# Sparse attention with a gated MLP on one core: the first half's global V rows by transfers, zeroing on GpSimd, casts on VectorE, and a changed order and banks around the first AV products

## The chip, the core and the metric

The kernel runs on one core of a Trainium2 chip. The metric is the device time of one execution in microseconds (us). Ten executions of the kernel before gave a median of 238.23 us (237.54 to 239.25).

## The reference

Two things are computed one after the other. First an attention over 4 batches, 8 heads, 768 positions and a head width of 64, in which a position sees the first 8 keys (the global ones) and the 96 keys up to itself, with a bias that falls with distance and has a slope of its own for each head. Then a gated MLP over the 3,072 resulting rows of width 512.

```python
scores = scale * np.matmul(q, k.transpose(0, 1, 3, 2))
is_global = pos[None, :] < n_global                      # 8
is_local = (rel >= 0) & (rel < n_local)                  # 96
dist = np.where(is_global & ~is_local, n_local, np.abs(rel))
scores = np.where(is_global | is_local, scores - slopes * dist, -1e9)
a = softmax(scores)
x = np.matmul(a, v)                                      # then (B*S, H*D)
out = (np.maximum(x @ w_gate, 0) * (x @ w_val)) @ w_out  # 512 -> 1536 -> 512
```

## The kernel before, in words

**Tiling.** The work is cut into eight half batches of 384 queries, numbered s = 0 to 7 in the code (`NHALF`). Each has four head pairs p = 0 to 3. The keys of a batch are held in seven blocks j of 128 columns: 8 global keys, the same in every block, and 120 local ones. A first half (s even) needs blocks 0 to 3, a second half blocks 2 to 6. `vbuf` holds V in the same blocks with keys on partitions: partitions 0 to 7 hold the global rows of V, repeated in every block, and partitions 8 to 127 the block's own rows.

**Stages of a half.** `piece_cast` (L258) turns q and k from fp32 to bf16. `piece_t` (L288) transposes them on TensorE. `piece_copy_k` and `piece_copy_q` (L304, L312) bring the transposed keys and queries from PSUM to `kT` and `qT`. `piece_bias` (L319) puts the bias into three PSUM banks by a matmul, `piece_scores` (L334) adds the scores, and `piece_exp` (L348) takes the exponential on ScalarE. `piece_av_wide` (L454) makes two products: the sums of the weights (with a tile of ones, `what` = 0), and then the weights times V (`what` = 1). `piece_ln_wide` and `piece_inverse_wide` (L481, L486) make the reciprocal of the sums as exp(-ln) on ScalarE. `piece_mul_wide` (L491) multiplies on VectorE into `xT`. The MLP reads `xT`: `gate` and `val` (L748, L756) are its first two matmuls with weights `wg` and `wv`, followed by a third product with `wo`.

**What sets the order.** The schedule is manual: every engine executes its instructions in the order in which the program calls the pieces, and waits by semaphores on what it reads and on the buffers that it overwrites. For the first two halves the order is written out by hand, from L834 to L977; from L978 on, lists of pieces are woven between the MLP's matmuls. PSUM has three pools: `qk` with 3 banks, `av` with 2 and `ff` with 3 (L76 to L78). A bank can be written again when its last reader is done. `rc_pool` (L70) has two buffers each for the logarithms and the reciprocals, so the fourth pair's reciprocal waits until the second pair's has been used.

**Queues.** SyncE issues the fp32 loads of q and k for the first half at once (L177). GpSimd issues all loads that cast to bf16: the global V rows (`load_v_globals`, L140), V blocks (`load_v`, L152), q and k of the second half (`load_qk_cast`, L126), and the weights (`load_w`, L170). It issues them in program order among its memsets.

**The places that the change touches.** `copy_v_globals` (L148) spreads the global rows of V over the blocks by VectorE copies, in two calls; it is used in the first batch only. For the later batches `spread_v_globals` (L144) does the same by six small transfers within SBUF, issued by SyncE (8 partitions x 8 heads x 64 elements each). `zero_values` (L205) zeroes partitions 32 to 127 of V's block 3 for the first batch, as only 24 of its rows are loaded early. The first AV product with its ln and inverse stands after the exponentials of the last head pair (L880, L881), the second half's first transposes after the third AV product (L904), and a second half's copies after the fourth (L907).

Of the kernel before, what the change touches and what calls it, by code (L numbers as in the profile page):

```python
# [16 lines left out]
def kernel(  # L17
# [12 lines left out]
    nc = tc.nc  # L30
# [15 lines left out]
    NT = -(-S // KT)  # L46
# [79 lines left out]
    def load_qk_cast(s, h0=0, h1=H):  # L126

        b, half = divmod(s, 2)
        for i, src in ((1, k), (0, q)):
            qk16[s, i] = kc[i].rearrange("p n d -> p (n d)").rearrange("p (h x) -> p h x", h=H)  # L130
            nc.gpsimd.dma_start(
                out=qk16[s, i][:, h0:h1],
                in_=src[b, h0:h1, half * QH : (half + 1) * QH, :].rearrange(
                    "h (p n) d -> p h (n d)", n=NN))

    def v_dst(b, r0, r1, j):
        t = vbuf[b % 2][r0:r1, j, D:]
        return t.rearrange("p (h z) -> p h z", z=2 * D)[:, :, 0:D]
# [5 lines left out]
    def spread_v_globals(b, j0=1, j1=NT):  # L144
        for j in range(j0, j1):
            nc.sync.dma_start(out=v_dst(b, 0, NG, j), in_=v_dst(b, 0, NG, 0))

    def copy_v_globals(eng, b, j0, j1):  # L148
        t = vbuf[b % 2][0:NG, :, D:].rearrange("p j (h z) -> p j h z", z=2 * D)[:, :, :, 0:D]
        eng.tensor_copy(t[:, j0:j1], t[:, 0:1].to_broadcast([NG, j1 - j0, H, D]))  # L150

    def load_v(b, j, r0=0, r1=KT):  # L152
        n = min(r1, S - KT * j) - r0
        nc.gpsimd.dma_start(  # L154
            out=v_dst(b, NG + r0, NG + r0 + n, j),
            in_=v[b, :, KT * j + r0 : KT * j + r0 + n, :].rearrange("h p d -> p h d"))
# [13 lines left out]
    def load_w(dst, src, f0, f1):  # L170
        nc.gpsimd.dma_start(out=dst, in_=src[:, f0:f1].rearrange("(c p) f -> p c f", p=128))
# [29 lines left out]
    def zero_keys():  # L201
        for p in range(1, HP):
            nc.vector.memset(kT[0][p][:, 3, 32:128], 0.0)

    def zero_values():  # L205
        for r0, r1 in ((32, 64), (64, 128)):
            nc.vector.memset(v_dst(0, r0, r1, 3), 0.0)

# [35 lines left out]
    def warm_up(n):  # L246
        wps = ff_psum.tile([128, 512], FP32, name="ff_ps")
        for _ in range(n):
            nc.tensor.matmul(wps, lhsT=warm, rhs=warm.unsqueeze(1).to_broadcast([128, 4, 128]), start=True, stop=True)

    QKB, FFB, AVB = (qk_psum, "qk_ps"), (ff_psum, "ff_ps"), (av_psum, "av_ps")
# [6 lines left out]
    def piece_cast(s, p, i, eng):  # L258
        if (s, p) not in cast_of:
            cast_of[s, p] = oflat[:, 384 * p : 384 * (p + 1)].bitcast(BF16).rearrange(  # L260
                "t (i n e d) -> t i n e d", i=2, n=NN, e=2)
        src = (qs_of[s], ks_of[s])[i]
        (eng.copy if eng is nc.scalar else eng.tensor_copy)(
            cast_of[s, p][:, i].rearrange("t n e d -> t e n d"),
            src[:, 2 * p : 2 * p + 2, :].rearrange("t e (n d) -> t e n d", n=NN))
# [22 lines left out]
    def piece_t(s, p, pool=av_psum, name="av_ps", apart=False):  # L288
        for i in (1, 0):
            if i == 1 or apart:  # L290
                tp = pool.tile([128, 512], FP32, name=name)
                tp = tp[:, 0:QH].bitcast(BF16).rearrange("d (i t) -> d i t", i=2)
            tp_of[s, p, i] = tp[:, i, :]
            for n in range(NN):
                for e in range(2 if s == 1 else 1):
                    r = slice(64 * e, 64 * e + 64) if s == 1 else slice(0, 128)
                    src = (qk16[s, i][:, 2 * p + e, n * D : (n + 1) * D] if s == 1
                           else cast_of[s, p][:, i, n])
                    nc.tensor.matmul(tp[r, i, n * 128 : (n + 1) * 128],  # L299
                                     lhsT=src, rhs=ident, is_transpose=True,  # L300
                                     start=((i == 1 or apart) and n == 0),
                                     stop=((i == 0 or apart) and n == NN - 1))

    def piece_copy_k(s, p):  # L304
        b, half = divmod(s, 2)
        put_keys(nc.vector.tensor_copy, nc.vector.tensor_copy, kT[b % 2][p], tp_of[s, p, 1], half)

    def piece_copy(s, p):
        piece_copy_k(s, p)
        piece_copy_q(s, p)  # L310

    def piece_copy_q(s, p, copy=nc.vector.tensor_copy):  # L312
        for e in range(2):
            r = slice(64 * e, 64 * e + 64)
            copy(qTb[s % 2][r, p, e, :], tp_of[s, p, 0][r, :])
# [45 lines left out]
    def piece_biased(s, p):  # L361
        piece_scores(s, p)
        for g in range(3):
            piece_exp(s, p, g)
# [89 lines left out]
    def piece_av_wide(s, p, *pools):  # L454

        b, half = divmod(s, 2)
        todo = [t for bank in banks_of_half[half] for t in bank]
        pools = pools or (AVB,)
        av = [pool.tile([128, 512], FP32, name=name) for pool, name in (pools[0], pools[-1])]
        for what in range(2):  # L460
            av3 = av[what][:, 0:QH].rearrange("d (n p) -> d n p", n=NN)
            for i, (j, a, w, m) in enumerate(todo):
                for e in range(2):
                    es, ce = es_of[s, p, j, e]
                    z0 = D + 2 * D * (2 * p + e)
                    nc.tensor.matmul(av3[64 * e : 64 * e + 64, :, a : a + w],  # L466
                                     lhsT=ones if what == 0 else vbuf[b % 2][:, j, z0 : z0 + D],
                                     rhs=es[:, ce : ce + NN * w].rearrange("k (n p) -> k n p", n=NN),
                                     start=(i == 0), stop=(i == len(todo) - 1),
                                     skip_group_check=True)  # L470
        av_of[s, p] = av
# [5 lines left out]
    def piece_sums_wide(s, p):  # L477
        piece_ln_wide(s, p)
        piece_inverse_wide(s, p)

    def piece_ln_wide(s, p):  # L481
        ln = rc_pool.tile([128, QH], FP32, name="lnd")
        nc.scalar.activation(ln, av_of[s, p][0][:, 0:QH], AF.Ln, bias=0.0, scale=1.0)
        av_of[s, p, "l"] = ln

    def piece_inverse_wide(s, p):  # L486
        rc = rc_pool.tile([128, QH], FP32, name="rcp")
        nc.scalar.activation(rc, av_of[s, p, "l"], AF.Exp, bias=0.0, scale=-1.0)
        av_of[s, p, "r"] = rc

    def piece_mul_wide(s, p):  # L491
        if s not in xT_of:
            xT_of[s] = xt_pool.tile([128, N_DC, QH], BF16, name="xT")
        nc.vector.tensor_tensor(xT_of[s][:, p, :], av_of[s, p][1][:, 0:QH], av_of[s, p, "r"], op=ALU.mult)
# [327 lines left out]
    def cast(s, p, ek, eq):  # L822
        piece_cast(s, p, 1, ek)
        piece_cast(s, p, 0, eq)

    V, P, A = nc.vector, nc.gpsimd, nc.scalar
# [14 lines left out]
    for j in range(3):  # L841
        load_v(0, j)
    load_v(0, 3, 0, 24)
    load_qk_cast(1, 0, H // 2)
    for f in (0, 256):
        load_w(wg[0][:, :, f : f + 256], moe_w_gate, f, f + 256)
    load_qk_cast(1, H // 2, H)
    load_w(wv[0], moe_w_val, 0, GW * 128)
    warm_up(7)
    cast(0, 0, V, V)  # L850
    piece_t(0, 0, apart=True)
    piece_bias(0, 0)
# [1 line left out]
    piece_copy_k(0, 0)  # L854
    piece_copy_q(0, 0, nc.scalar.copy)
    zero_keys()
    zero_values()
    cast(0, 1, A, V)
    piece_scores(0, 0)
    piece_t(0, 1)  # L860
    piece_bias(0, 1)
    piece_exp(0, 0, 0)
    cast(0, 2, A, A)
    piece_exp(0, 0, 1)
    piece_exp(0, 0, 2)
    piece_copy(0, 1)
    piece_t(0, 2)
    cast(0, 3, A, A)
    piece_biased(0, 1)
    piece_bias(0, 2, (0, 1))  # L870
    piece_copy(0, 2)
# [2 lines left out]
    piece_biased(0, 2)  # L874
    piece_copy(0, 3)
    piece_bias(0, 3)
    copy_v_globals(V, 0, 1, 4)
    piece_biased(0, 3)
    copy_v_globals(V, 0, 4, NT)
    piece_av_wide(0, 0, QKB)  # L880
    piece_sums_wide(0, 0)  # L881

    zero_q(P, 1)
    for p in range(HP):
# [9 lines left out]
        piece_copy(s, p)  # L894

    gate, val = F0[0:8:2], F0[1:8:2]
    piece_av_wide(0, 1)
    piece_ln_wide(0, 1)
    piece_av_wide(0, 2, FFB)
    piece_ln_wide(0, 2)  # L900
    piece_mul_wide(0, 0)
    piece_inverse_wide(0, 1)
    piece_inverse_wide(0, 2)
    piece_t(1, 0, *QKB)  # L904
    piece_av_wide(0, 3, QKB, FFB)
    piece_ln_wide(0, 3)
    piece_copy(1, 0)  # L907
    piece_mul_wide(0, 1)
    piece_inverse_wide(0, 3)
    piece_t(1, 1)  # L910
    piece_bias(1, 0)
    piece_mul_wide(0, 2)
    piece_mul_wide(0, 3)
    piece_copy(1, 1)
    for h in (3, 4):
# [123 lines left out]
```

## Time and profile before

| what | us |
|---|---|
| median of ten executions | 238.23 |
| the profiled execution | 239.25 |
| its span | 237.4 |
| TensorE (PE) busy in the span | 231.0 (97%) |
| VectorE (DVE) busy | 188.1 (79%) |
| ScalarE (ACT) busy | 146.2 (62%) |
| GpSimd (POOL) busy | 90.4 (38%) |
| granted TensorE clock | full in all 40 slices |
| DMA moved | 30.43 MB, mean 128 GB/s |

The profile is one execution; its own time is the span and what lies around it (1.85 us). An engine's busy time is an average over stages with different limits: the stage that the change touches is the first 31 us. In the first 4 us TensorE is busy for 3.0 us, and from 16 to 18 us for 1.39 of 2 us. In the rows of a timeline the first number is the start within the span, the second the length, and brackets hold the idle time before the row and what ended it. POOLq and SPq are the queues that issue transfers; q0 is the DMA queue of GpSimd's transfers and q1 that of SyncE's. A share of 100% in a DMA row means all 16 DMA engines; it can be above that, since packets overlap on an engine.

### The profile page before, as it was taken

What the parts mean: (1) busy time and instruction counts of PE and PEld (TensorE: products, weight loads), DVE (VectorE), ACT (ScalarE), POOL (GpSimd) and SP (SyncE); (2) the same over time, 40 slices, a digit from 0 to 9 for tenths busy, and PEclk for the clock granted to TensorE, in tenths of its full rate; (3) what the DMA queues carried; (4) which work ended last, traced back from release to release, by engine and by line L of the source; (5) the groups of instructions that cost most, each with busy time, mean ns of one, the idle gap of its engine ahead of it and who ended that gap; (6) DMA issues with size and microseconds to landing.
All of it is one profiled execution on the core that took longest, in us unless ns stands there. A gap on an engine that the chain in (4) does not pass through costs nothing.

```text
span 237.4 us, 5510 instructions
## 1 busy us (share of the span) xinstructions
PE 231.0 (97%) x2021; PEld 159.2 (67%) x2021; DVE 188.1 (79%) x466; ACT 146.2 (62%) x321; POOL 90.4 (38%) x191
## 2 busy tenths in 40 slices
PE   7989999999999999999999999999999999999994
PEld 3776666656677666856688566856688666865683
DVE  5688767869977878976989788876889777873784
ACT  6899875667623887567842687558742687624310
POOL 8998903933565065606580065505150000000000
PEclk9999999999999999999999999999999999999999
DMA  6999999998469974767398664847712200020005
GB/s 170 201 167 183 206 270 274 169 109 266 46 134 188 169 246 95 64 160 227 90 77 123 189 204 105 53 125 244 78 45 88 91 0 3 0 91 0 1 3 177
DMA packets 71419, 30.43 MB, mean 128 GB/s; under 512 B 47744, under 2 KB 70784, under 8 KB 71392
## 3 DMA queue, kind: packets, MB, share of 16 engines
q0 software_dynamic: 34896, 10.27, 38.9%
q1 hardware_dynamic: 36496, 19.82, 30.7%
q8 instruction: 16, 0.26, 0.5%
q14 instruction: 11, 0.09, 0.1%
HBM read 28.38 MB, written 6.29 MB: 146 GB/s over the span
## 4 chain that ended last, share of the span: by engine, by line
PE 85%; ACT 6%; DVE 5%; DMA 1%; issue 1%; SPq 0%; DVEq 0%; ACTq 0%
PE ff_ps L744 50%; PE ff_ps L632 19%; PE av_ps L431 5%; PE ff_ps L777 2%; PE av_ps L513 2%; PE qk_ps L513 2%; DVE obuf L643 1%; DMA qs<-in_q_dram 1%; PE av_ps L299 1%; PE qk_ps L344 1%; DVE xT L451 1%; ACT grelu L753 1%; ACT rcp L445 1%; PE av_ps L466 1%; ACT lnd L440 1%
## 5 line engine op out<-in xcount | busy, mean ns | idle before, releaser
L753 ACT ACTIVATE grelu<-ff_ps 128x384 bf16<-128x384 f32 x96 | 46.8, 490 | 53.2 <-PE ff_ps L744 40.8
L744 PE MATMUL ff_ps<-xT,wv 128*128 128x384 bf16 x384 | 77.9, 326 | 0.0
L744 PE MATMUL ff_ps<-xT,wg 128*128 128x384 bf16 x384 | 77.7, 326 | 0.1
L760 DVE TENSOR_TENSOR ht<-ff_ps,grelu 128x384 f16<-128x384 f32 x96 | 53.3, 556 | 25.4 <-PE ff_ps L744 22.0
L744 PEld LDWEIGHTS <-wv 128*128 128x128 bf16 x384 | 36.0, 98 | 23.7 <-issue 1.2
L744 PEld LDWEIGHTS <-wg 128*128 128x128 bf16 x384 | 36.4, 97 | 21.8 <-issue 1.4
L451 DVE TENSOR_TENSOR xT<-av_ps,rcp 64x384 bf16<-64x384 f32 x48 | 26.6, 555 | 7.7 <-ACT rcp L445 6.7
L367 POOL CAST kc<-ks 128x384 bf16<-128x384 f32 x20 | 10.8, 583 | 53.7 <-DMA ks<-in_k_dram 53.7
L534 DVE TENSOR_TENSOR es<-es,m_all 128x432 bf16<-128x432 bf16 (+3 forms) x108 | 30.7, 328 | 0.2 <-ACT es L522 0.2
L643 DVE TENSOR_TENSOR obuf<-ff_ps,obuf 128x512 f32<-128x512 f32 (+1 forms) x46 | 27.6, 603 | 3.7 <-PE ff_ps L632 0.9
L440 ACT ACTIVATE lnd<-av_ps 64x384 f32<-64x384 f32 x48 | 23.3, 485 | 11.3 <-PE av_ps L431 10.5
L522 ACT ACTIVATE es<-qk_ps 128x432 bf16<-128x432 f32 (+2 forms) x54 | 27.6, 531 | 0.0
L154 POOL DMA_DIRECT2D vbuf<-in_v_dram x29 | 24.8, 864 | 0.1
L431 PE MATMUL av_ps<-es,vbuf 128*128 128x216 bf16 (+4 forms) x216 | 21.4, 226 | 0.2 <-DVE xT L451 0.2
L431 PEld LDWEIGHTS <-vbuf 128*128 128x128 bf16 x216 | 18.2, 98 | 5.0 <-issue 0.3
L632 PEld LDWEIGHTS <-ht 128*128 128x128 f16 x198 | 18.6, 97 | 3.9 <-issue 0.8
L632 PEld LDWEIGHTS <-hsum 128*128 128x128 f16 x192 | 18.5, 98 | 2.1
L632 PE MATMUL ff_ps<-wo_sb,ht 128*128 128x256 f16 x132 | 19.3, 272 | 0.0
L632 PE MATMUL ff_ps<-wo_sum,hsum 128*128 128x256 f16 x144 | 17.2, 273 | 0.0
L445 ACT ACTIVATE rcp<-lnd 128x384 f32<-128x384 f32 x24 | 12.6, 523 | 0.8
L367 POOL CAST qc<-qs 128x384 bf16<-128x384 f32 x20 | 10.5, 568 | 0.7 <-DMA qs<-in_q_dram 0.5
L522 ACT ACTIVATE es<-av_ps 128x432 bf16<-128x432 f32 (+2 forms) x18 | 9.5, 528 | 1.8 <-PE qk_ps L513 1.8
(130 smaller groups left out, 265.4 us busy)
## 6 DMA issues: line engine op xcount, KB each, us to landing
out_dram<-obuf SPq DMA_DIRECT2D x22, 256.0 KB
ks<-in_k_dram SPq DMA_DIRECT2D x5, 768.0 KB
qs<-in_q_dram SPq DMA_DIRECT2D x5, 768.0 KB
vbuf<-in_v_dram POOLq DMA_DIRECT2D x23, 120.0 KB, 4.6
wv<-in_moe_w_val_dram POOLq DMA_DIRECT2D x3, 512.0 KB, 10.2
wo_sb<-in_moe_w_out_dram POOLq DMA_DIRECT2D x1, 1536.0 KB, 21.2
wg<-in_moe_w_gate_dram POOLq DMA_DIRECT2D x2, 512.0 KB, 9.8
ks<-in_k_dram SPq DMA_DIRECT2D x4, 192.0 KB
```

The source lines that it names most:

```text
L154: nc.gpsimd.dma_start(out=v_dst(b, NG + r0, NG + r0 + n, j), in_=v[b, :, KT * j + r0 : KT * j + r0 + n, :].rearrange("h p d -> p h d"))
L367: nc.gpsimd.tensor_copy(dst[s % 2].rearrange("t n (h d) -> t h n d", d=D)[:, 2 * p : 2 * p + 2], src[s][:, 2 * p : 2 * p + 2, :].rearrange ...
L431: nc.tensor.matmul(av3[:, :, a : a + w], lhsT=vb[:, j, z0 : z0 + 128], rhs=es[:, c : c + NN * w].rearrange("k (n p) -> k n p", n=NN), star ...
L440: nc.scalar.activation(ln[o0 : o0 + 64], av[d0 : d0 + 64, 0:QH], AF.Ln, bias=0.0, scale=1.0)
L451: nc.vector.tensor_tensor(xT_of[s][r, p, :], av_of[s, p, e][r, 0:QH], av_of[s, p, "r"][r], op=ALU.mult)
L522: nc.scalar.activation(es[:, 0:cols], ps[:, 0:cols], AF.Exp, bias=0.0, scale=scale)
L534: nc.vector.tensor_mul(e4, e4, mk)
L632: nc.tensor.matmul(ps[:, c0 : c0 + DH], lhsT=lhs(i), rhs=rhs(i), start=(i == 0), stop=(i == NP - 1), skip_group_check=True)
L643: add = lambda o, x, y: nc.vector.tensor_tensor(o, x, y, op=ALU.add)
L744: nc.tensor.matmul(st[key][:, 0:QH], lhsT=w_of(w, dc, fc), rhs=xT_of[c][:, dc, :], start=(dc == 0), stop=(dc == N_DC - 1))
L753: nc.scalar.activation(gr, psg[:, 0:QH], AF.Relu, bias=0.0, scale=1.0)
L760: nc.vector.tensor_tensor(ht[:, fc, :], psv[:, 0:QH], st["r", fc], op=ALU.mult)
```

## The change

The two `copy_v_globals` calls go, and `spread_v_globals(0)` is called instead, right after the warm-up matmuls, so that its six transfers follow the q and k loads on SyncE. The zeroing of block 3 goes from VectorE to GpSimd, and to a place ahead of the second half's loads. The key casts of head pairs 2 and 3 go from ScalarE to VectorE. The first AV product, with its ln and inverse, stands ahead of the fourth pair's scores and exponentials; its sums go to an `av` bank instead of a `qk` bank. The product of head pair 0 with its reciprocal, and the transposes and copies of the second half's pair 0, move up. The fourth pair's sums go to an `av` bank as well, and the transposes of the second half's pair 1 move down by two pieces.

```diff
     def zero_values():
         for r0, r1 in ((32, 64), (64, 128)):
-            nc.vector.memset(v_dst(0, r0, r1, 3), 0.0)
+            nc.gpsimd.memset(v_dst(0, r0, r1, 3), 0.0)
...
     load_v(0, 3, 0, 24)
+    zero_values()
     load_qk_cast(1, 0, H // 2)
...
     warm_up(7)
+    spread_v_globals(0)
     cast(0, 0, V, V)
...
     zero_keys()
-    zero_values()
     cast(0, 1, A, V)
...
-    cast(0, 2, A, A)
+    cast(0, 2, V, A)
...
-    cast(0, 3, A, A)
+    cast(0, 3, V, A)
...
     piece_bias(0, 3)
-    copy_v_globals(V, 0, 1, 4)
+    piece_av_wide(0, 0, AVB, QKB)
+    piece_sums_wide(0, 0)
     piece_biased(0, 3)
-    copy_v_globals(V, 0, 4, NT)
-    piece_av_wide(0, 0, QKB)
-    piece_sums_wide(0, 0)
...
     gate, val = F0[0:8:2], F0[1:8:2]
+    piece_mul_wide(0, 0)
     piece_av_wide(0, 1)
     piece_ln_wide(0, 1)
+    piece_t(1, 0, *QKB)
+    piece_copy(1, 0)
     piece_av_wide(0, 2, FFB)
     piece_ln_wide(0, 2)
-    piece_mul_wide(0, 0)
     piece_inverse_wide(0, 1)
     piece_inverse_wide(0, 2)
-    piece_t(1, 0, *QKB)
-    piece_av_wide(0, 3, QKB, FFB)
+    piece_av_wide(0, 3, AVB, FFB)
     piece_ln_wide(0, 3)
-    piece_copy(1, 0)
     piece_mul_wide(0, 1)
     piece_inverse_wide(0, 3)
-    piece_t(1, 1)
     piece_bias(1, 0)
     piece_mul_wide(0, 2)
+    piece_t(1, 1)
     piece_mul_wide(0, 3)
     piece_copy(1, 1)
```

## The prediction

> **What bounds the kernel now.** I read the chain that ended last first, then the timelines of GpSimd, VectorE and SyncE over the first 31 us, then the DMA packets in narrow windows. In the chain each row is start, length and engine with its line:
>
> ```profile
> 12.66 0.38 DVE qT L315
> ...
> 13.08 0.36 PE ff_ps L344
> 13.46 1.30 ACT kN L359 x3
> ...
> 17.55 0.57 DVE xT L494
> ...
> 18.21 0.52 ACT rcp L488
> 18.73 0.91 ACT m_all L244 x2
> 19.64 1.33 ACT es L359 x3
> 20.97 1.14 ACT grelu L753 x3
> 22.11 1.35 ACT es L400 x3
> ...
> 23.85 1.30 PE ff_ps L744 x8
> ...
> 31.14 9.86 PE ff_ps L744 x60
> ```
>
> The reader is to see three stretches. Until 13.08 TensorE and VectorE alternate. From 13.46 to 23.5 ScalarE carries the chain. From 23.85 TensorE does, back to back. So a gain or loss in the first 31 us is worth what it shifts TensorE there, and what shifts it stays to the end, as nothing later in the chain has slack of that size to give. The page has TensorE at 97%: all its idle time is 6.4 us, and that caps any gain.
>
> The other stream runs beside this. GpSimd issues all casting loads in order, and from 7 us to 31 us the DMA engines never pause: the window answers put q0 above 100% in every stretch and steadily at 200 to 210 GB/s at the end. GpSimd's timeline:
>
> ```profile
> 8.10 0.79 POOL L131 DMA_DIRECT2D kc<-in_k_dram  x1
> ...
> 15.56 0.55 POOL L886 MEMSET vbuf<- 64x544 uint32 x1
> ```
>
> Landings, each the issue start plus the trace's issue-to-landing: V's globals 4.05+4.8 = 8.85; V block 3 (24 rows) 7.5+3.8 = 11.3; first keys and queries of the second half (kc, qc) 13.3 and 14.3; second kc and qc 18.3 and 20.2; wv0 12.56+10.2 = 22.76; wg1 27.9; wv1 20.67+9.8 = 30.47. TensorE asks for second qc at 20.87 (the query half of L299 from 20.74), for wv0 at 23.51, for wg1 near 28.85, for wv1 at 31.07. The slacks are thus 0.67, 0.75, 0.95 and 0.6 us. They are what the change can use up.
>
> **Part by part.** *VectorE.* The two copies (L150, 1.77 us at 13.05) and two memsets (L207, 0.64 at 5.88) go. After the copies VectorE sat 0.90 us waiting for the reciprocal, and before the next key copy it sat longer:
>
> ```profile
> 8.42 0.53 DVE L278 COPY kT<-av_ps 128x360 bf16<-128x360 bf16 x1 [1.51 <-PE av_ps L299]
> ```
>
> So both removals take away hidden work: 0 on the path. Two key casts come on, 0.36 each (rows of L263 on VectorE). The first fits that 1.51 us hole. The second meets 0.28 us of idle before 10.07, so at about 0.33 start to start it costs 0.05; if its hole were gone, 0.33.
>
> *ScalarE* loses 2 x 0.51 = 1.02 us of casts before 9.7, but then it waits for scores that wait for VectorE's qT copies (0.37, 0.25 and 0.19 idle before its three exponential groups). Nothing is gained there. The reordering does fill the last gap: ln and reciprocal of head pair 0 (0.51+0.52) run at 13.3 to 14.25, before the last exponentials, which then run 14.25 to 15.55. Ln of pair 1 comes at about 15.4, not 15.60.
>
> *Banks and order.* Before, bias of the next half waits for ln of pair 3 (TensorE idle 0.61 to 17.70), and VectorE does pair 0's product and the key copies at 15.72 to 17.5, so pair 1's product starts at 17.55 and the reciprocal of pair 3, which reuses its buffer, only at 18.21. After, pair 0's product is done by 14.9 and the transposes go ahead of the second AV product, so copies run 15.7 to 17.1, pair 1's product ends near 17.65, and the reciprocal starts there: up to 0.55 us earlier than 18.21. The bank wait itself only moves: transposes of pair 1 now wait for pair 3's ln. That costs nothing while ScalarE is the chain, since its next two masks (0.91) cover it; without them it would be about 0.3.
>
> *The six transfers.* They sit on SyncE's queue behind the q and k loads; SyncE waits for the globals at 8.85, and queued behind that wait is nothing until 47 us. But TensorE now waits for three of them in its AV product, and behind that product stand the scores of pair 3 in the same order, and behind them ScalarE. The same six transfers of the next batch are in SyncE's timeline, and behind it the packets (count, MB, share) that each queue moved between 50.0 and 50.4:
>
> ```profile
> 47.41 5.25 SPq L146 DMA_DIRECT2D vbuf<-vbuf  x6
> ```
>
> ```profile
> q0 software_dynamic: 420, 0.05, 208.0%
> q1 hardware_dynamic: 19, 0.00, 7.6%
> ```
>
> With q0 full, q1 moves some 20 per 0.4 us. Each transfer is 64 packets, 192 for the three needed. From the first issue (47.41) they were through at about 51.9, with q0 thinning from 51.2. Completion comes some 0.5 us after the last packet (first keys: packets through by 2.8, cast at 3.36). Call L the landing of the third. As in the trace: 8.9+4.5+0.5 = 13.9. With q0 full all along: first packets 2.25 us after issue, then 192/20 x 0.4 = 3.8, so 15.4. Unloaded, as the sixth transfer (gone 1.6 us after its issue): 8.9+1.8+1.6+0.5 = 12.8. The Trainium skill, "DMA: Bandwidth & Descriptors", section on the anatomy of one DMA, puts a fixed cost near 2 us on a transfer, with the bytes on top; 8 KB is then 2.0 us and L an estimated 12.7, wholly hidden, where the row under load gives 13.9 to 15.4. I take 14.2, near the loaded row, as the two first transfers meet a gap (below). In the walk above, the last exponentials start at the later of 14.25 and L+0.43, and the reciprocal 3.2 us after that; L = 14.2 gives 17.83, a gain of 0.38. L = 14.6 breaks even, L = 12.7 gives the full 0.55, L = 15.4 loses 0.8.
>
> *Two memsets on GpSimd* stand ahead of the second half's loads. Nearest rows: 544 words 0.55 us (L886), 288 words 0.29 (L159). Each has 512 bf16 elements: 0.5 each, 1.0 together; 0.26 each if packed in pairs, as VectorE's row has them (0.55 together). Seven loads and then everything GpSimd issues stand behind. Is the delay hidden by a backlog? Counted up window by window, V's 3,136 packets (392 rows of 8 heads) run out at about 10.1 to 10.3, and first kc packets start then, 2.0 us after its issue. So there is almost no backlog at that moment: about 0.2 us. After it there is one without end up to 31 us, so a gap at 10.3 is never made up. Delay of all later landings: 1.0-0.2 = 0.8. The 384 packets of the spread take turns with q0, 26 ns each (7.6% of 16 engines over 0.4 us, by 19): between 0 and 0.6 us more, partly in the gap; I take 0.3. Call the delay S: 1.1, between 0.35 and 1.5.
>
> *A rule against the casts.* The Trainium skill, "SBUF — State Buffer", section on the two separate sides, says that a VectorE copy of fp32 within SBUF locks GpSimd out of a shared port, so that it cannot write descriptors meanwhile. By that the two moved casts could hold GpSimd's issue by up to 2 x 0.36 = 0.7 us, and S would be 1.8. The row: the cast of L263 at 6.54 to 6.90 ran beside a V issue at 6.6 that took 0.911 us, as the one before it did (0.911), and another 0.932. I take 0.
>
> **The sum.** Second qc: 20.2+1.1 = 21.3 against 20.87, so TensorE stalls and a ScalarE gain of 0.38 dies here; ScalarE had some 0.2 in hand, leaving +0.25. wv0: 22.76+1.1 against 23.51 = +0.35. wg1: 29.0 against 28.85 = +0.15. wv1: 31.57 against 31.07 = +0.5. These are not added: each is how late TensorE is against before, and the last and largest stays. The queries of the next batch land 39.64+1.1, cast 0.5 later, asked for at about 41.0+0.5: no more. So +0.5 us. The profiled execution took 239.25, of which 237.4 are the span and 1.85 lie around it; it is 1.02 above the median. On the span it is 237.9, on the median 238.23+0.5 = 238.7.
>
> **Rivals.** *The DMA stream decides* (forecast, 0.42): 238.7, and 238.0 to 239.1 over S from 0.35 to 1.5. *The spread decides* (0.16): L at 15.4 stops TensorE, then ScalarE, and the reciprocal comes 0.8 late; with the DMA delay's lesser slack behind it 239.0 to 239.6. For it: 20 packets per 0.4 us. Against: the gap at 10.3. *The gain reaches the end* (0.20), the other side: memsets at 0.26 each and small packets that cost q0 nothing give S = 0.35, every slack above it, and ScalarE's earlier reciprocal carries through: 238.23-0.4 to -0.55 = 237.7 to 237.85. It decides from S below about 0.3 to 0.6. For it: landings have the slack listed. Against: no backlog at 10.3. *Nothing shows* (0.22): gain eaten at second qc, delay within the slacks (S near 0.6): 238.2.
>
> **How the numbers follow.** Some 0.2% (0.48 us) is what measurement can tell from no change. Of the forecast 0.34 lies beyond it and 0.08 within; of the spread case all 0.16 is slower; of the gain case 0.15 faster, 0.05 within; the last 0.22 within, less 0.01 to faster. Faster 0.16, same 0.34, slower 0.50. Range 237.7 to 239.5: it takes in the gain case and all of the spread case but its end.
>
> **What would show it.** kc's first issue at about 9.1, not 8.10, with two GpSimd memsets of about 0.5 before it; landing of second qc past 21 and wv1 past 31.3; a TensorE wait at L299 near 21 and at L744 near 31. The third spread's landing shows in when the scores of pair 3 start (13.1 if hidden, about 14.2 as taken, 15.4 at worst), the ScalarE gain in the start of pair 3's reciprocal (17.8 against 18.21). Wrong would be: memsets of 0.2, loads landing where they did, or TensorE held at the AV product beyond 14.6.

## The result, and the profile after

The changed kernel is slower: 239.1 us median of 15 runs (238.09 to 239.92), beside 237.84 for the kernel before (52 runs, 237.06 to 239.27). The ratio is 1.0047, with an interval from 1.0033 to 1.0061, that is +1.1 us; the forecast had +0.5. The profiled execution took 240.09 us with a span of 238.3, longer than any of those 15 runs; the profile of before is the longest of its first ten (239.25). In e2, e4 and e8 below TensorE's clock falls in some or all of the executions, and the ratios of e4 and e8 leave out those that lost over 1.5% by it, so their medians stand beside them.

The page after, first the busy times, then the two DMA queues:

```profile
PE 229.5 (96%) x2021; PEld 157.9 (66%) x2021; DVE 185.1 (78%) x464; ACT 145.9 (61%) x319; POOL 90.5 (38%) x193
...
q0 software_dynamic: 34896, 10.27, 38.4%
q1 hardware_dynamic: 36928, 19.86, 31.2%
```

VectorE has lost 3.0 us of work (188.1 before) and GpSimd has gained two instructions. q1 has 432 packets more, among them the 6 x 64 of the spread. TensorE does the same 2,021 matmuls in a span that is 0.9 us longer. The chain that ended last shows a different start:

```profile
4.07 4.99 DMA vbuf<-in_v_dram
9.07 0.90 SPq L146
10.02 0.68 SPq L146
10.75 4.16 DMA vbuf<-vbuf
15.05 0.20 PE qk_ps L466 x2
15.25 0.62 PE ff_ps L344 x4
...
18.06 0.51 ACT rcp L488
18.57 0.39 ACT lnd L483
19.00 0.53 PE av_ps L299 x12
...
20.22 1.95 PE ff_ps L744 x12
...
32.46 9.86 PE ff_ps L744 x60
```

From 13.46 to 23.5 us the chain of before ran mostly over ScalarE, with VectorE's rows near 16 and at 17.55 between. Now it runs, up to 15.05, over a load of V's global rows and then one 8 KB transfer that takes 4.16 us. Pair 3's scores start at 15.25 in the chain, the long run of 60 MLP matmuls at 32.46 where it was 31.14. TensorE's timeline has the place; in brackets stands the wait and what ended it:

```profile
12.42 0.50 PE L466 MATMUL qk_ps<-es,vbuf 128*64 128x216 bf16 x4
13.87 0.25 PE L466 MATMUL qk_ps<-es,vbuf 128*64 128x144 bf16 x2 [0.94 <-DMA vbuf<-vbuf]
15.05 0.20 PE L466 MATMUL qk_ps<-es,vbuf 128*64 128x24 bf16 x2 [0.93 <-DMA vbuf<-vbuf]
15.18 0.69 PE L344 MATMUL ff_ps<-qT,kT 128*128 128x432 bf16 x4
```

The AV product takes its blocks one by one and stops for the second and the third transfer: 1.87 us in all, behind which the scores stand. Of GpSimd's stream, the two memsets and the first key load:

```profile
8.19 1.10 POOL L207 MEMSET vbuf<- 32x512 bf16 x2
9.23 0.79 POOL L131 DMA_DIRECT2D kc<-in_k_dram  x1
```

That load is issued 1.13 us later than before (8.10), as forecast. What was forecast from it is not in this profile: the first and second queries of the second half land at 14.1 and 19.85 (14.3 and 20.2 before), wv0 at 22.6 (22.76), wv1 at 30.85 (30.47). None of these loads stops TensorE. So the profile shows the rival in which the spread decides, while the forecast had the loads. That had to be told apart.

### The profile page after: what moved, and what is told of

Read it like the earlier page. It is cut to its first block, busy times and chain, and to the rows that moved or that the text cites. A ratio compares the mean times of both kernels' runs of the same rounds, so it can differ in the third digit from the quotient of the medians.

```text
span 238.3 us, 5524 instructions
## 1 busy us (share of the span) xinstructions
PE 229.5 (96%) x2021; PEld 157.9 (66%) x2021; DVE 185.1 (78%) x464; ACT 145.9 (61%) x319; POOL 90.5 (38%) x193
## 4 chain that ended last, share of the span: by engine, by line
PE 89%; DMA 4%; ACT 2%; DVE 1%; POOL 1%; issue 1%; SPq 1%; POOLq 0%; DVEq 0%
PE ff_ps L744 53%; PE ff_ps L632 19%; PE av_ps L431 6%; PE ff_ps L777 2%; PE av_ps L513 2%; DMA vbuf<-in_v_dram 2%; DMA vbuf<-vbuf 2%; PE qk_ps L513 2%; DVE obuf L643 1%; PE av_ps L466 1%; PE qk_ps L299 1%; SPq L146 1%; ACT es L400 1%; PE qk_ps L466 1%; PE av_ps L299 1%
## 5 line engine op out<-in xcount | busy, mean ns | idle before, releaser
L534 DVE TENSOR_TENSOR es<-es,m_all 128x432 bf16<-128x432 bf16 (+3 forms) x108 | 30.1, 323 | 0.2 <-ACT es L522 0.2
L431 PE MATMUL av_ps<-es,vbuf 128*128 128x216 bf16 (+4 forms) x216 | 21.4, 226 | 0.0
L632 PE MATMUL ff_ps<-wo_sb,ht 128*128 128x256 f16 x132 | 19.2, 272 | 0.0
L367 POOL CAST qc<-qs 128x384 bf16<-128x384 f32 x20 | 10.3, 556 | 0.7 <-DMA qs<-in_q_dram 0.4
```

What stands on the lines that cost most here:

```text
L367: nc.gpsimd.tensor_copy(dst[s % 2].rearrange("t n (h d) -> t h n d", d=D)[:, 2 * p : 2 * p + 2], src[s][:, 2 * p : 2 * p + 2, :].rearrange ...
L431: nc.tensor.matmul(av3[:, :, a : a + w], lhsT=vb[:, j, z0 : z0 + 128], rhs=es[:, c : c + NN * w].rearrange("k (n p) -> k n p", n=NN), star ...
L534: nc.vector.tensor_mul(e4, e4, mk)
L632: nc.tensor.matmul(ps[:, c0 : c0 + DH], lhsT=lhs(i), rhs=rhs(i), start=(i == 0), stop=(i == NP - 1), skip_group_check=True)
```

## The experiments

Each kernel was timed against the kernel before. A ratio of 1.001 is 0.24 us.

**Theory T1, rivals T2 and T3.** T1: the loss is what the profile after shows, TensorE stopped in the first AV product by the transfers. T2: the forecast's stream; two memsets on GpSimd make every casting load late, and that is the loss. T3: the new order and banks cost by themselves. The first four kernels ask for T1 and T2.

**e1: the changed kernel, with the VectorE copies in place of the transfers.**

```diff
     warm_up(7)
-    spread_v_globals(0)
...
+    copy_v_globals(V, 0, 1, 4)
     piece_av_wide(0, 0, AVB, QKB)
     piece_sums_wide(0, 0)
     piece_biased(0, 3)
+    copy_v_globals(V, 0, 4, NT)
```

> The changed kernel with one part undone: the six transfers go, and the two VectorE copies of V's global rows stand where they stood, the first of them now just ahead of the first AV product. Order, banks, casts and GpSimd's zeroing stay as changed. Theory T1 (TensorE is held at the first AV product until the third transfer lands, 15.0 us in the changed kernel's profile): the AV product's V part starts by about 14 us, no wait on a transfer is left, and the time falls by 1 us or more against the changed kernel, to between 0.4 us below the kernel before and its own time (ratio 0.998 to 1.000). Rival T2 (the memsets on GpSimd make all later loads late): no change against the changed kernel, ratio 1.0047. Rival T3 (the new order and banks: the transposes of pair 1 wait for pair 3's ln): ratio 1.003 or more.

Measured: 1.0037 (1.0024 to 1.0050), +0.9 us. Most of the loss stays without any transfer, so T1 by itself, which expected 1.000 or less, falls; T2 and T3 are not told apart here. The kernel is less clean than was meant, since the copies now make TensorE wait 0.91 us at the same place. At 30.90 it waits for wv1, as T2 has it, though by 0.24 us only:

```profile
13.09 0.36 PE L466 MATMUL qk_ps<-es,vbuf 128*64 128x216 bf16 x6 [0.91 <-DVE vbuf L150]
30.90 0.82 PE L744 MATMUL ff_ps<-xT,wv 128*128 128x384 bf16 x4 [0.24 <-DMA wv<-in_moe_w_val_dram]
```

**e2: the changed kernel, with the three needed transfers behind the other three.**

```diff
-    spread_v_globals(0)
+    spread_v_globals(0, 4, NT)
+    spread_v_globals(0, 1, 4)
```

> The changed kernel with the six transfers in another order: blocks 4, 5, 6 first, then 1, 2, 3. The same transfers, bytes and packets. T1: the last transfer that the first AV product needs is now the sixth instead of the third; with some 1.4 us per transfer (first to third landing in the changed kernel) it lands about 3 to 4 us later, near 18 to 19 us, and the time rises by 2.5 to 4 us above the changed kernel, ratio 1.015 to 1.022. T2 and T3: no change, ratio 1.0047.

Measured: 1.0292 (1.0259 to 1.0326), 244.67 us: 5.8 us above the changed kernel, for the same bytes in another order. TensorE stops for 2.22, 0.44 and 1.74 us, and the third needed transfer lands near 17.1, so that pair 3's scores start 2.2 us later than in the changed kernel. Part of the rest is the clock: TensorE's granted clock is 0.50 from 16 to 20 us and 0.53 from 20 to 22, and it falls in all six executions (means of 0.986 to 0.993). So the 5.8 us are the wait and what followed it, which this run does not separate. Once the AV product waits for them, the transfers are on the path.

**e3: the kernel before, with only the zeroing moved to GpSimd, ahead of the second half's loads.**

```diff
-            nc.vector.memset(v_dst(0, r0, r1, 3), 0.0)
+            nc.gpsimd.memset(v_dst(0, r0, r1, 3), 0.0)
...
     load_v(0, 3, 0, 24)
+    zero_values()
     load_qk_cast(1, 0, H // 2)
...
     zero_keys()
-    zero_values()
```

> The kernel before with one part of the change alone: the zeroing of V's block 3 by GpSimd ahead of the second half's loads. T1: the loads are issued 1.1 us later but land at most 0.6 us later (as in the changed kernel's trace), within the slack of 0.6 to 0.95 us: ratio 0.999 to 1.001. T2: it carries most of the 1.1 us, ratio 1.003 to 1.005. The prediction's own step (landings late by 1.1 us): ratio 1.002.

Measured: 1.0023 (1.0011 to 1.0036), +0.55 us. This is the forecast's step by itself, at the forecast's size. TensorE's weight loads stand still where it said, at second qc, wv0 and wv1:

```profile
19.86 0.53 PEld L299 LDWEIGHTS <-kc 128*64 128x64 bf16 x18 [0.25 <-DMA kc<-in_q_dram]
22.47 1.20 PEld L744 LDWEIGHTS <-wv 128*128 128x128 bf16 x8 [0.22 <-DMA wv<-in_moe_w_val_dram]
30.14 0.44 PEld L744 LDWEIGHTS <-wv 128*128 128x128 bf16 x4 [0.27 <-DMA wv<-in_moe_w_val_dram]
```

That is no proof of late loads. The same three waits stand in e9 below, whose zeroing is on VectorE, whose loads are issued as before and whose time is that of before:

```profile
20.37 0.53 PEld L299 LDWEIGHTS <-kc 128*64 128x64 bf16 x18 [0.33 <-DMA kc<-in_q_dram]
22.96 1.21 PEld L744 LDWEIGHTS <-wv 128*128 128x128 bf16 x8 [0.21 <-DMA wv<-in_moe_w_val_dram]
30.66 0.44 PEld L744 LDWEIGHTS <-wv 128*128 128x128 bf16 x4 [0.29 <-DMA wv<-in_moe_w_val_dram]
```

In both profiles TensorE gets there 0.4 to 1.0 us earlier than in that of before, and the loads land much as before. In e3 second qc, wv0 and wv1 land at 19.8, 22.4 and 30.1, no later than before. Its profiled execution (237.57) is also the fastest of its 22, below the median of before. So the price of the step is measured by time, and how it arises is not shown.

**e4: the changed kernel, with the zeroing back on VectorE** (the diff of e3 the other way).

> The changed kernel with the zeroing back on VectorE in its old place, so that the second half's loads are issued 1.1 us earlier again. T1: the small transfers now have no gap in GpSimd's stream and meet the load packets throughout, so the third lands no earlier and perhaps up to 0.5 us later: ratio 1.0047 to 1.007. T2: the loss goes, ratio 1.000 or below.

Measured: 1.0089 (1.0056 to 1.0122) and a median of 243.08, with executions from 238.75 to 244.27. Taking away the part that costs 0.55 us by itself made it worse. The profiled execution (242.58) shows why. TensorE first, then four stretches of 2 us: length, busy time of PE, PEld, DVE, ACT and POOL (instructions in brackets), granted clock, DMA share, GB/s.

```profile
13.54 0.25 PE L466 MATMUL qk_ps<-es,vbuf 128*64 128x144 bf16 x2 [1.11 <-DMA vbuf<-vbuf]
15.16 0.23 PE L466 MATMUL qk_ps<-es,vbuf 128*64 128x24 bf16 x2 [1.37 <-DMA vbuf<-vbuf]
15.32 1.18 PE L344 MATMUL ff_ps<-qT,kT 128*128 128x432 bf16 x4
```

```profile
12.00:14.00 2.00, 0.68 (x14) 0.33 (x8) 0.00 (x0) 1.28 (x3) 1.96 (x3) 1.00 1.40 160
14.00:16.00 2.00, 0.84 (x4) 0.44 (x5) 0.50 (x1) 0.10 (x1) 1.85 (x8) 0.72 1.42 177
16.00:18.00 2.00, 2.00 (x29) 1.71 (x29) 0.06 (x1) 1.68 (x4) 2.00 (x3) 0.50 1.64 194
18.00:20.00 2.00, 2.00 (x50) 1.89 (x44) 1.54 (x6) 1.25 (x4) 1.13 (x3) 0.93 1.30 209
```

The waits are 0.6 us longer in all than in the changed kernel. The transfers were issued 1 us earlier (first at 8.06, not 9.07), but the third one releases TensorE at 15.16, beside 15.05 there. In the changed kernel the memsets leave a gap in GpSimd's stream: from 10.4 to 11.6 us q0 has 369 packets there, and 675 in e4. That fits small transfers that go faster through the gap. Then the granted clock falls to 0.50: the four score matmuls take 1.18 us, not 0.69, and from 16 to 18 us TensorE gets 29 matmuls done. In the changed kernel the same stretch reads:

```profile
16.00:18.00 2.00, 2.00 (x61) 1.95 (x58) 1.04 (x5) 2.00 (x6) 1.91 (x8) 1.00 1.57 188
```

Each execution's mean granted clock says how much of e4 this is. In three of its 13 executions it is 0.998 or more; they took 238.75, 238.98 and 239.82. In the other ten it is 0.986 to 0.993, and they took 240.64 to 244.27. In the 16 executions of the changed kernel it is never under 0.997. The three are within the range of the changed kernel (238.09 to 239.92), so the excess of the ten goes with the clock. They are not below it either: with the transfers in, taking the memsets off GpSimd shows no gain, and T2 alone falls.

**e8: the kernel before, with only the transfers in place of the copies.**

```diff
     warm_up(7)
+    spread_v_globals(0)
...
-    copy_v_globals(V, 0, 1, 4)
...
-    copy_v_globals(V, 0, 4, NT)
```

> The kernel before with the six transfers in place of VectorE's two copies, and nothing else of the change: the first AV product stays behind the fourth pair's scores, zeroing on VectorE. T1: the third transfer lands near 15 to 15.5 while the product is due at about 12.7 to 14, but its scores and exponentials are already through, so only TensorE and ln wait: ratio 1.004 to 1.010, more if TensorE runs at half rate after the wait, as in the profiles of the runs with the transfers in the other order and with the zeroing back on VectorE (4 matmuls of L344 in 1.18 us instead of 0.67). If the transfers do no harm by themselves: 0.999 to 1.001.

Measured: 1.0097 (1.0068 to 1.0127), +2.3 us, median 240.53. TensorE waits 0.89 and 0.87 us at the AV product, as in the changed kernel, but its clock is 0.50 from 16 to 18 us. Of 11 executions four had a mean clock of 1.0; they took 238.71 to 239.99. Even these are above the 237.74 of the kernel before in the same comparison. The transfers alone are the dearest single part that was tried.

**e7: the kernel before, with the zeroing on GpSimd done twice.** It is e3 with the call of `zero_values` doubled; the second pair of memsets writes the same zeros.

> The kernel before with the zeroing on GpSimd done twice, so that the second half's loads are issued 2.2 us later instead of 1.1 (the second pair of memsets writes the same zeros). If the loads' slack was used up by the first pair, which gave 0.55 us, the second adds its full 1.1: ratio 1.006 to 1.0075. If the first pair cost its 0.55 in some other way (GpSimd and VectorE in each other's way) the second adds the same again: 1.0045. If 1.0023 was chance: 1.001 to 1.003.

Measured: 1.0057 (1.0025 to 1.0089), +1.4 us. The first key load is issued at 8.10 before, 9.25 in e3 and 10.38 here, and the time goes up by 0.55 and then by 0.8. Here loads do land late and stop TensorE: second qc at 21.4, wv0 at 24.2 and wv1 at 31.8, with waits at second qc, wg, wv0 and wv1 of 0.85, 0.55, 0.49 and 0.27 us. So T2's mechanism is seen with two pairs of memsets. For one pair it is not: with seven executions the interval takes in 1.0045, twice e3's excess, which was expected if the memsets cost in some other way, for instance by hindering VectorE.

**e6: the changed kernel, with the load of V's global rows issued ahead of the bias tables.** The transfers can then start early.

```diff
+    load_v_globals(0)
     nc.gpsimd.iota(rel, ...
...
-    load_v_globals(0)
```

> The changed kernel with one line moved: the load of V's global rows is issued by GpSimd ahead of the bias tables, 2.7 us earlier, and the tables come 0.74 us later. T1: the six transfers start some 2 to 3 us earlier, the third lands by about 12.5, TensorE's wait at the first AV product is gone, and the loss falls to that of the late loads and the order, ratio 1.002 to 1.0037. If only the loads decide: ratio 1.0047 as before.

Measured: 1.0038 (1.0024 to 1.0053). SyncE issues the transfers from 4.97 on, and the AV product runs through:

```profile
12.73 0.43 PE L467 MATMUL qk_ps<-es,vbuf 128*64 128x216 bf16 x8
```

A wait of 1.87 us in the profile is gone, and the gain is not measurable (1.0038 and 1.0047, intervals overlapping). Something else stands close behind; which it is, this run does not show. One price is the edit's own: the first key load is issued at 9.57, 0.34 later than in the changed kernel.

**e5: e1 with the zeroing on VectorE as well**, so that only the order, the banks and the two casts are left of the change.

> The first experiment (the changed kernel with VectorE's copies instead of the six transfers) and, besides, the zeroing back on VectorE. What is left of the change is the order, the banks and the two casts. Theory so far: two limits stand side by side, TensorE's order up to the first AV product (the third transfer) and the loads behind GpSimd's memsets; zeroing alone gave 1.0023, the change without the transfers 1.0037. If order and banks cost something by themselves, ratio 1.001 to 1.002 (what is left of 1.0037 without 1.0023). If they bring a gain that the late loads hid, ratio 0.996 to 0.999.

Measured: 1.0018 (1.0005 to 1.0031), +0.4 us. So these three parts are not free together, by a small margin.

**e9: e5 with the two key casts back on ScalarE**, so that order and banks are left.

```diff
-    cast(0, 2, V, A)
+    cast(0, 2, A, A)
...
-    cast(0, 3, V, A)
+    cast(0, 3, A, A)
```

> The kernel of the fifth experiment (order, banks and casts alone, 1.0018) with the two key casts back on ScalarE, so that only order and banks are left. If the second cast costs the loss (it stands on VectorE between two runs of key and query copies, and took 0.58 us there in the fifth experiment's profile, with no idle time before it in the profile of zeroing alone): ratio 0.999 to 1.000. If the order does (transposes of pair 1 behind pair 3's ln, gate at 18.06 us against 17.37 in the profile of zeroing alone): ratio 1.0015 to 1.0025. The prediction's step (the order gains 0.38 us): 0.998.

Measured: 1.0000 (0.9985 to 1.0015). The order and the banks neither gain nor lose 0.4 us. Beside e5 that would put the 0.4 us on the casts, but the two intervals overlap.

**e10: e6 with the zeroing on VectorE, and e12: e10 with the key casts on ScalarE.**

> The changed kernel with V's global rows loaded early, as in the sixth experiment (1.0038), and the zeroing back on VectorE. T1: the transfers run before the load stream is dense, so putting the loads back in time takes off the zeroing's share and brings no loss at the first AV product: ratio 1.001 to 1.002, where the same step without the early load (fourth experiment) made it 1.0089. If the transfers themselves cost, wherever they stand: 1.003 or more.

> The tenth experiment (changed order and banks, V's global rows loaded early and spread by the transfers, zeroing on VectorE; 1.0019) with the two key casts back on ScalarE. If the casts cost 0.0018 here too, as between the fifth and the ninth experiment: ratio 0.999 to 1.001. If VectorE, now free of copies as well, has become faster than the kernel before: 0.997 to 0.9985. If the casts' price was chance: 1.0015 to 1.002.

Measured: e10 1.0019 (1.0001 to 1.0036), e12 1.0030 (1.0016 to 1.0043). From e6 to e10 the zeroing gives back 0.45 us, with intervals that overlap. Moving the casts back gave nothing (the intervals overlap), so a price of the casts, which e5 and e9 suggested, is not confirmed. e12 is e9 but for the transfers and the early load. The two intervals do not meet, and e12's AV product does not wait for a transfer. In its profile the first key load is issued at 8.51 (8.11 in e9), and TensorE waits for the first queries:

```profile
14.36 0.20 PEld L300 LDWEIGHTS <-kc 128*64 128x64 bf16 x6 [0.53 <-DMA kc<-in_q_dram]
```

So 0.7 us go even where the transfers are early; which share their packets have, and which the earlier load, these runs do not separate.

**e11: the kernel before, with the second weight group loaded in halves, gate and value in turn.**

```diff
-    load_w_group(1)
+    for f in (0, 256):
+        for w, m in ((wg, moe_w_gate), (wv, moe_w_val)):
+            load_w(w[1][:, :, f : f + 256], m, GW * 128 + f, GW * 128 + f + 256)
```

> The kernel before with the second weight group loaded in halves of 256 columns, gate and value in turn, so that the first half of wv1, which TensorE asks for at about 30 to 31 us, is issued third from its neighbours' data half a transfer (about 2.5 us) earlier. Same bytes. If the load stream is a limit of the kernel before already (TensorE waited for wv1 in the profiles with the order alone and with the zeroing alone): ratio 0.997 to 0.999. If TensorE's own order is the limit there, and the stream only becomes one when it is delayed: 0.999 to 1.001.

Measured: 1.0002 (0.9983 to 1.0022). No gain; in its profile TensorE still waits 0.6 us for wv. No version here beats the kernel before.

## Why the prediction was near in time, and only partly right in cause

**The sum.** From the kernel before, the parts one on top of the other (ratio less one, times 237.8 us):

| what is in | ratio | us |
|---|---|---|
| order and banks (e9) | 1.0000 | 0.0 |
| and the two casts (e5) | 1.0018 | +0.4 |
| and the zeroing on GpSimd (e1) | 1.0037 | +0.9 |
| and transfers for copies (the change) | 1.0047 | +1.1 |

Neighbouring intervals overlap, so no single row of this ladder is certain. The rows were also not timed side by side: beside e9 the kernel before had a median of 238.13, beside e1 and e5 237.77 and 237.74. The zeroing's step is seen three times, +0.55 alone (e3), 0.45 from e5 to e1 and 0.45 from e10 to e6, but only in the first does the interval lie clear of no change.

That the time fell into 237.7 to 239.5 says little, since that range held nearly all of the four cases. The +1.1 us are over twice the forecast's +0.5 and lie in the range of the spread case, 239.0 to 239.6, to which the prediction gave 0.16.

**The memsets and the DMA stream.** The sizes were right, and the step between them is not borne out. The memsets took about 0.5 us each, as taken, the first load was issued at 9.23 as forecast (9.1), and the cost by itself is e3's +0.55. In between the prediction has every later landing late by S = 1.1 us, because a gap at 10.3 is never made up. The gap was there (306 packets fewer than in e4 from 10.4 to 11.6), and it was made up: in the changed kernel's profile the landings run from 0.35 early (second qc) to 0.5 late (wg1, 28.4 for 27.9). Over the profiles with no memset of V on GpSimd second qc lands at 19.2 to 20.4, with one pair of them at 19.8 to 20.3. Only two pairs (e7) bring it past 21. So loads that land where they did, one of the prediction's signs of being wrong, came true, and the path by which one pair costs 0.5 us stays open.

**L, the third transfer.** Mis-sized: taken as 14.2, measured 15.0, inside the bounds of 13.9 to 15.4 and near the worst. By the prediction's own sum, in which 14.6 breaks even, that is a loss of some 0.4 us and no gain, and TensorE held at the product beyond 14.6 was its other sign of being wrong. The transfers are issued 0.75 us apart, but the second releases TensorE at 13.87 and the third at 15.05, 1.2 us apart. Without the gap in q0, in e4, L was 15.2 after an issue that was 1 us earlier. The Trainium skill's fixed cost near 2 us, which its section gives for transfers issued by GpSimd and which the prediction set against the loaded row, would have had the transfers hidden at an estimated 12.7; these, issued by SyncE beside a full q0, took up to 4.16 us, so here the row decides.

**The gain of 0.38 on ScalarE.** The reciprocal did come earlier, and it was not what TensorE hangs on. e9 has the new order without any transfer or memset, and its time is that of before. From the scores of the third pair (p = 2) on, first in the kernel before and then in e9:

```profile
11.59 0.67 PE L344 MATMUL qk_ps<-qT,kT 128*128 128x432 bf16 x4
17.16 0.49 ACT L483 ACTIVATE lnd<-qk_ps 128x384 f32<-128x384 f32 x1
18.21 0.52 ACT L488 ACTIVATE rcp<-lnd 128x384 f32<-128x384 f32 x1 [0.55 <-DVE xT L494]
18.69 2.11 PE L744 MATMUL ff_ps<-xT,wg 128*128 128x384 bf16 x12
```

```profile
10.49 0.67 PE L344 MATMUL qk_ps<-qT,kT 128*128 128x432 bf16 x4
16.21 0.48 ACT L483 ACTIVATE lnd<-av_ps 128x384 f32<-128x384 f32 x1
16.72 0.52 ACT L488 ACTIVATE rcp<-lnd 128x384 f32<-128x384 f32 x1
16.74 0.53 PE L299 MATMUL av_ps<-ident,kc 128*64 128x128 bf16 x12 [0.24 <-ACT lnd L483]
17.80 2.11 PE L744 MATMUL ff_ps<-xT,wg 128*128 128x384 bf16 x12
```

Counted from those scores the reciprocal of pair 3 starts 0.39 us earlier in e9 (6.23 for 6.62), just what was forecast. But the ln of pair 3 starts 0.15 later (5.72 for 5.57), as pair 0's ln and reciprocal now stand ahead of it. That ln frees the bank for which TensorE waits, before for the bias (0.61 us) and now for the transposes of pair 1 (0.24), and TensorE's first gate matmul comes 0.21 later (7.31 for 7.10). So the clause that failed is that the bank wait costs nothing while ScalarE is the chain: TensorE stands behind the ln, and in e9 ScalarE later waits 0.53 us for TensorE's scores (L397). Why e9 is not slower by those 0.2 us is open; its next stop is the second queries, for which its weight load waits 0.33 us.

**The copies taken off VectorE.** As work that was hidden they were rightly put at 0; but with the AV product moved up TensorE waits for them (0.91 us in e1, 0.42 in e5, 0.45 in e9). The change needs either them or the transfers at that place. What the wait for the copies is worth at the end was not measured apart; e9 has it and takes the time of before.

**The second cast.** The hole it was to fit in was that of one long execution. In it the matmuls of the first 10 us take 1.7 times as long as in the changed kernel, though its row of granted clock is full in all slices. The first bias in the profile of before, and then in that of the changed kernel:

```profile
5.32 1.21 PE L329 MATMUL qk_ps<-obuf,wo_sum 128*128 128x216 bf16 x8
```

```profile
4.48 0.70 PE L329 MATMUL qk_ps<-obuf,wo_sum 128*128 128x216 bf16 x8
```

From the first pair's scores to the third's it takes 5.01 us in before (6.58 to 11.59) and 3.92 in e8, e9 (6.57 to 10.49) and other profiles. So VectorE's holes there, and the slacks of the loads, were read from a stretch that others run faster. In e5 the cast meets no idle time and is long:

```profile
8.63 0.58 DVE L263 CAST obuf<-ks 128x384 bf16<-128x384 f32 x1
9.24 0.53 DVE L278 COPY kT<-av_ps 128x360 bf16<-128x360 bf16 x1
```

It takes 0.6 us from start to start, not the 0.05 of the prediction nor its fallback of 0.33. Whether this reaches the end stays open: by time e5 and e9 say 0.4 us, e10 and e12 say nothing or the reverse. In the profiles of e5 and e9 the delay is gone by 21.00 us, where both start the same scores (L397), since e9 has waited for the second queries. What e5 loses against e9 in these profiles comes later, in its longest execution of 22, by a wait of 0.91 us for a load of V at 27.22.

**The rule on the shared port.** The prediction gave it 0, and GpSimd's issues did keep their length (0.77 to 0.79 us in the changed kernel). The disturbance is on VectorE: that cast, 0.36 us elsewhere, took 0.58 here and 0.65 at 7.08 in the changed kernel. Whether GpSimd's work beside it is the cause was not tried alone.

**Verdict.** The direction is shown, and so is the price of the memsets by themselves, near half of the whole. How the memsets reach the end is not shown. The rest, some 0.6 us, lies in what was put at nothing or at a gain: the transfers that hold TensorE, and perhaps the casts. That the time came out in the range is thus in part luck. The parts do not add up: alone transfers and memsets cost 2.3 (with what the clock's falls add) and 0.55, together with the rest 1.1. With transfers and memsets TensorE keeps its full clock in all 16 executions; without the memsets, in e4 and e8, it loses it in most. Why is open.

## What to carry to other kernels

A small transfer under a dense stream of loads takes what the loaded row says, not its bytes; before a matmul is made to wait for one, count the packets beside it and look for a gap. Compute on the engine that issues the loads makes every load behind it be issued later; whether it also lands later is to be read from the landings. Slacks and waits of a quarter of a microsecond depend on which execution was profiled: compare its time with the median, and see whether a kernel without the edit shows the same wait. Where two edits hold the same engine at different places, undo each alone and add each alone, since here taking one part away (e4) brought a bigger loss.

## What the runs showed of the hardware that was not expected

TensorE's granted clock fell to 0.50 after a stretch in which it was waiting but not idle. In e4 it fell at 14.9 us; in the 3.4 us before, TensorE was busy for 1.22 us, 0.25 of them in the last 2. In e8 it fell at 15.6, after 1.65 us busy of 3.4, and in e2 at 15.1, after 0.80. It stayed at half for about 3.4 us in e4 and e8 and for twice that in e2. The changed kernel's profile has TensorE busy for at least 1.54 us in any 3.4 us there, and in none of its 16 executions did the clock fall. The Trainium skill, "TensorE: Matmul & The Clock Gate", section on the clock gate, has the half rate follow an idle window of about 3.4 us that runs freely against the kernel. That it differs between executions, ten of 13 in e4 and seven of 11 in e8, and that it lasts 3.4 us or twice that agree with it; a wholly idle window was not needed here. Where the limit lies is open, as e8 was busier than the changed kernel and fell.

Pace and granted clock can part in the first microseconds: matmuls took 1.21 us for eight in before and 0.70 in the changed kernel, both with a granted clock of 1.00 in the profile. The cause is open.

The order of six 8 KB transfers was worth 5.8 us (e2); 2.2 of them are the later start of pair 3's scores, and a half clock follows. And an edit that took 1.87 us of waits out of the profile (e6) was worth nothing that could be measured.
